# A top-1 expert kernel: the rows 384 to 511 of an expert in float32 blocks of 64 rows, sums of the weights, and a new order

## Chip, cores and metric

The kernel runs on one core of one Trainium2 chip. The metric is the device time of one execution in microseconds (us). The input is one fixed random draw.

## What is computed

Attention in a window of 64 positions (4 batches, 8 heads, 576 positions of 64 channels) gives 2304 tokens of 512 channels. They go through a dense layer pair with `g = h - tanh(h)` (512 to 2048 to 512), and then each token through one of eight experts.

```python
h = x @ w_in                              # 2304 x 512 x 2048
x = (h - np.tanh(h)) @ w_out              # 2304 x 2048 x 512
xn = x / (np.linalg.norm(x, axis=-1, keepdims=True) + 1e-06)
en = expert_emb / (np.linalg.norm(expert_emb, axis=-1, keepdims=True) + 1e-06)
logits = xn @ en.T / tau
expert_idx = np.argmax(logits, axis=1)
...
gate_w = probs[np.arange(N), expert_idx]
for e in range(E):
    mask = expert_idx == e
    h = np.maximum(x[mask] @ w1[e], 0.0)                  # w1[e]: 512 x 1024
    out[mask] = gate_w[mask, None] * (h @ w2[e])          # w2[e]: 1024 x 512
```

With the input of the runs the experts get, in the order in which the kernel takes them, 446, 369, 345, 167, 389, 154, 253 and 181 tokens.

## The kernel before

**Products.** Nearly all products are made of three: an operand is split into a rounded high part and the rest (VectorE subtracts, ScalarE or VectorE rounds), and `mm3` (lines 659 to 662) sums high by high, high by low and low by high. A weight buffer `w` holds the high parts of two 512-column pieces in columns 0 to 1023 and the low parts in 1024 to 2047 (`t_split_w`, line 941). Attention and the token logits use plain float32 products, those of attention on halves of the array (`pv`, line 588, at line 593), those of the logits on quarters (`lg`, line 842, at line 845).

**Order.** A planner, `Sched` (line 83), takes tasks with an engine, a cost, a priority, what they read and write, and the buffers that they need, and writes the instructions of all engines in the order in which they would start. `SHIFTS` is a table of numbers, one for a task, that moves priorities in the first stretch. [...]

**The straight part.** Attention, the dense pair, the routing and the first 256 rows of expert 0 are planned together, up to the first branch (on hardware: to 546 us). The routing (`t_route`, line 784) takes 256 tokens at a time: logits (line 845), turned by line 855, VectorE's choice of the expert (lines 871 to 881), counting products (`ps_`, lines 901 to 904), and a scatter by GpSimd that writes every token's number and gate to its expert's list `lst` (line 927). Lists are loaded by SyncE (`t_list`, line 1333), made into row numbers by VectorE (`t_ids`, lines 987 and 988), and the token rows are gathered by GpSimd (`t_gather`, line 1001) into buffers `v` (rows 0 to 255) or `g` (rows 256 to 511).

**An expert.** Stage e of the loop at line 1467 runs the first 256 rows of expert e (`t_ffn`, line 1074: `h` products of 256 columns, a relu and a split, `o` products of 512 columns), loads and splits the weights of expert e+1, and gathers. `t_out` (line 1112) scales an output by its gate on ScalarE (line 1119) or VectorE (line 1120) into a buffer `pr`, and GpSimd scatters it to `out` (line 1125). Behind that a branch (line 1490, "over") runs the second block, rows 256 to 383, if the expert has over 256 tokens: `t_xin1` (line 1134) transposes and splits the tokens, `t_ffn1` (line 1155) makes `a<-w,x` products, transposes (line 1186), a split (lines 1195 and 1199) and `o<-w,gh` products. Inside it a second branch (line 1501) does the same for the third block, rows 384 to 511. If the first test fails, an Else part prepares the next expert.

```python
with tc.If(vals[e] > CT + P):
    t_ffn1(ws, blk_o, 1, x_o, SC.now)
    SC.run()
```

**The end.** Behind the last expert `nov`, the number of blocks left over (none here), is loaded (line 1584), and a branch (line 1585) jumps over the code for them. [...]

## Time and profile before

| | before |
|---|---|
| median of 3 runs | 808.05 us (807.89 to 809.17) |
| profiled execution | 805.82 us |
| its span | 804.0 us |
| granted TensorE clock, mean | 0.993 |
| busy: TensorE, VectorE, ScalarE, GpSimd | 763.6, 582.8, 472.9, 90.9 us |
| memory traffic over the span | 134 GB/s |

The profile is of one execution. A busy time is the time in which an engine has an instruction in work; an idle time is put down to what ended it. The span runs from the first to the last instruction. In rows of a timeline the time in brackets is idle time ahead of the instruction, with what released it.

### The profile page before, as it was taken

The page shows a single profiled execution, that of the slowest core. Times are in us where ns is not written, and L with a number is a line of the kernel's source. Part 1 is how long each engine was busy: PE and PEld are TensorE (multiplying, and loading weights), DVE is VectorE, ACT ScalarE, POOL GpSimd, SP SyncE. Part 2 cuts the span into 40 slices and gives each one's busy share as a digit, 9 for nine tenths or more (in the row PEclk, how much of TensorE's full clock was granted, in tenths as well). Part 3 has the DMA queues.
Part 4 walks back from the last instruction along what each step waited for, and adds up shares of the span by engine and source line. Part 5 has one row for each costly group of instructions (what it writes and reads, how often), then busy time and mean ns, then how long its engine had stood idle before and what let it go on. Part 6 is the DMA issues. An engine that isn't in the chain of part 4 may idle for free. (4 is left out here: it accounts for less than half of the span.)

```text
span 804.0 us, 15561 instructions
## 1 busy us (share of the span) xinstructions
PE 763.6 (95%) x5703; PEld 672.4 (84%) x5703; DVE 582.8 (72%) x1482; ACT 472.9 (59%) x1121; POOL 90.9 (11%) x116
## 2 busy tenths in 40 slices
PE   4799999999999999999999999998999998999995
PEld 3687888898988789899989889887788888888994
DVE  6999999999988875857668689962282836815761
ACT  6999998889756765645646548721242424423440
POOL 3000000000001210010001011011122122102221
PEclk9999999999999999999999999999999999999998
DMA  9767746566534320200100018635082828523740
GB/s 294 241 188 214 241 148 223 160 216 212 161 106 122 95 80 22 71 1 2 53 1 27 27 34 292 218 61 157 20 247 83 259 62 282 169 82 104 255 132 24
DMA packets 65006, 108.27 MB, mean 135 GB/s; under 512 B 8452, under 2 KB 42244, under 8 KB 64912
## 3 DMA queue, kind: packets, MB, share of 16 engines
q1 hardware_dynamic: 60016, 93.93, 37.1%
q0 software_dynamic: 4896, 13.13, 5.1%
q8 instruction: 54, 0.88, 0.5%
q14 instruction: 40, 0.33, 0.1%
HBM read 88.00 MB, written 20.09 MB: 134 GB/s over the span
## 5 line engine op out<-in xcount | busy, mean ns | idle before, releaser
L660 PE MATMUL h<-x,w 128*128 128x256 f32 x688 | 198.5, 289 | 1.2 <-DVE g L715 1.1
L661 PE MATMUL h<-x,w 128*128 128x256 f32 x688 | 194.7, 283 | 2.0 <-DVE x L635 2.0
L662 PE MATMUL h<-x,w 128*128 128x256 f32 x688 | 194.6, 283 | 1.4 <-DVE w L447 1.4
L660 PE MATMUL o<-w,gh 128*128 128x512 f32 x436 | 175.2, 402 | 0.0
L662 PE MATMUL o<-w,gh 128*128 128x512 f32 x436 | 171.1, 393 | 0.9 <-DVE gh L729 0.7
L661 PE MATMUL o<-w,gh 128*128 128x512 f32 x436 | 170.9, 392 | 0.0
L660 PEld LDWEIGHTS h<-x,w 128*128 128x128 f32 x688 | 131.4, 191 | 8.2 <-issue 2.6
L661 PEld LDWEIGHTS h<-x,w 128*128 128x128 f32 x688 | 131.5, 191 | 4.8 <-DVE x L635 2.2
L662 PEld LDWEIGHTS h<-x,w 128*128 128x128 f32 x688 | 131.4, 191 | 1.6 <-DVE w L447 1.6
L662 PEld LDWEIGHTS o<-w,gh 128*128 128x128 f32 x436 | 81.9, 188 | 21.4 <-DVE gh L729 2.1
L660 PEld LDWEIGHTS o<-w,gh 128*128 128x128 f32 x436 | 82.2, 188 | 16.4 <-issue 2.0
L661 PEld LDWEIGHTS o<-w,gh 128*128 128x128 f32 x436 | 82.3, 189 | 13.8 <-DVE w L447 0.4
L276 ACT CAST w<-st 128x512 fp32r<-128x512 f32 x119 | 72.2, 633 | 22.7 <-DMA st<-in_moe_w_dram 15.2
L950 DVE TENSOR_TENSOR w<-st,w 128x512 fp32r<-128x512 f32 x128 | 83.3, 683 | 0.7
L706 DVE TENSOR_TENSOR g<-h,g 128x512 f32<-128x512 f32 x72 | 49.4, 686 | 29.0 <-ACT g L694 28.9
L1064 ACT ACTIVATE gh<-h 128x256 fp32r<-128x256 f32 x48 | 18.0, 383 | 76.8 <-PE h L662 60.6
L725 ACT CAST gh<-g 128x512 fp32r<-128x512 f32 x72 | 44.0, 620 | 28.3 <-DVE g L719 21.6
L690 ACT ACTIVATE g<-h 128x512 f32<-128x512 f32 x72 | 42.9, 596 | 26.5 <-PE h L662 26.4
L543 ACT ACTIVATE pr<-pr,mx 128x128 f32<-128x128 f32 x144 | 56.1, 401 | 3.2 <-DVE mx L534 3.2
L729 DVE TENSOR_TENSOR gh<-g,gh 128x512 fp32r<-128x512 f32 x72 | 48.6, 683 | 12.9 <-ACT gh L725 12.8
L698 ACT ACTIVATE g<-g,sqa 128x512 f32<-128x512 f32 x72 | 52.3, 726 | 7.2 <-DVE g L719 4.2
L1068 DVE SCALAR_TENSOR_TENSOR gh<-h,gh 128x256 fp32r<-128x256 f32 x48 | 19.8, 420 | 49.5 <-ACT gh L1064 38.6
(205 smaller groups left out, 1366.6 us busy)
## 6 DMA issues: line engine op xcount, KB each, us to landing
st<-in_moe_w_dram SPq DMA_DIRECT2D x64, 512.0 KB
st<-in_moe_w_in_dram SPq DMA_DIRECT2D x16, 512.0 KB
st<-in_moe_w_out_dram SPq DMA_DIRECT2D x16, 512.0 KB
v<-in_v_dram SPq DMA_DIRECT2D x16, 512.0 KB
part<-st SPq DMA_DIRECT2D x11, 512.0 KB
st<-part SPq DMA_DIRECT2D x11, 512.0 KB
k<-in_k_dram SPq DMA_DIRECT2D x16, 320.0 KB
q<-in_q_dram SPq DMA_DIRECT2D x18, 256.0 KB
```

The lines of the kernel that those rows point to most:

```text
L276: return {ACT: (act, lambda: nc.scalar.copy(out=o(), in_=i())), DVE: (dve, lambda: nc.vector.tensor_copy(out=o(), in_=i()))}
L543: nc.scalar.activation(out=pr_.t[:, i, :], in_=pr_.t[:, i, :], func=AF.Exp, bias=st["m"][:, i:i + 1], scale=-1.0, accum_out=st["den"][:, i ...
L660: nc.tensor.matmul(out=ps, lhsT=ah, rhs=bh, start=start, stop=False)
L661: nc.tensor.matmul(out=ps, lhsT=ah, rhs=bl, start=False, stop=False)
L662: nc.tensor.matmul(out=ps, lhsT=al, rhs=bh, start=False, stop=stop)
L690: {ACT: (0.49, lambda: nc.scalar.activation(out=u(), in_=hp.t, func=AF.Square))},
L698: {ACT: (0.62, lambda: nc.scalar.activation(out=sq(), in_=u(), func=AF.Square, scale=SQ_S, bias=sqa))},
L706: {DVE: (0.6, lambda: nc.vector.tensor_tensor(out=th(), in0=hp.t, in1=th(), op=ALU.subtract))},
L725: {ACT: (0.52, lambda: nc.scalar.copy(out=gh(), in_=sq()))}, reads=[(gq, 0), (acc[0], "-"), (acc[1], "-")],
L729: {DVE: (0.6, lambda: nc.vector.tensor_tensor(out=gl(), in0=sq(), in1=gh().bitcast(F32), op=ALU.subtract))},
L950: return lambda: eng.tensor_tensor(out=w.t[:, b], in0=raw.t[:, a], in1=w.t[:, a].bitcast(F32), op=ALU.subtract)
L1068: {DVE: (0.335, lambda: nc.vector.scalar_tensor_tensor(out=part(gs, 1), in0=hp.t[:, 0:CT], scalar=0.0, in1=part(gs, 0).bitcast(F32), op0=A ...
```

## The change

1. **Third block.** The test for rows over 384 now holds a block of 64 rows (`t_ffn_half`), and a test for rows over 448 inside it a second. A block of 64 rows uses plain float32 products with 64 columns of stationary data and 256 moving columns; the two halves of a 512-column row of weights go to output partitions 0 to 63 and 64 to 127, and the output rows, 256 columns wide, are scattered as half rows by numbers that `t_listh` makes.
2. **Sums.** These products need the weights in one piece, so `t_whole` adds high and low parts on VectorE: those of the first layer in the second block, into two `v` and two `pr` buffers; those of the second layer in the third block, into four `g` buffers and, when the first products have read them, the two `v` buffers. The second block's output goes to a `q` buffer.
3. **Hint.** TensorE is told of the test for 384 rows.
4. **End.** `nov` is loaded ahead of the last expert; ScalarE, VectorE and GpSimd are told of the last two branches. In the last expert the last two pieces of the hidden layer are multiplied out half of the rows by half (`last=2`).
5. **Order.** Three planner costs, `FAR` and the whole of `SHIFTS` are new, so all of the straight part stands in a new order.

```diff
-    -617, -89, -188, -90, -232, 135, -108, -84, -118, -93, -65, -74, -74, -76, 12, -30, -48, -70, 95, -705,
+    -1917, -29, -667, -400, -818, -83, -252, -353, -325, -373, -95, -86, -177, -233, 7, 51, -31, 79, 37, -1695,
...
-        SC.add({POOL: (1.04, sc)}, reads=[("su", c), ("pg", c)], writes=[("lst", 0)], prio=pr, lat=2.0)
+        SC.add({POOL: (1.4, sc)}, reads=[("su", c), ("pg", c)], writes=[("lst", 0)], prio=pr, lat=2.4)
...
+            if f < KF2 - last:
+                SC.part()
+                SC.add(
+                    {PE: (1.39, lambda p2=p2: p2((0, 1)))}, reads=rk, writes=[(acc[0], 0), (acc[1], 0)],
+                    allocs=acc if f == 0 and got else [], prio=pr + f + 1.5,
+                )
+            else:
+                ends.append((rk, p2))
         for i in range(2):
+            for rk, p2 in ends:
+                SC.add(
+                    {PE: (0.7, lambda p2=p2, i=i: p2((i,)))}, reads=rk, writes=[(acc[i], 0)], prio=pr + KF2 + i,
+                )
...
+    def t_whole(ws, at, keys, pr, late=()):
+        for n, (j, h) in enumerate(keys):
...
+                nc.vector.tensor_tensor(
+                    out=flat(f)[:, c:c + 512], in0=w.t[:, a].bitcast(F32), in1=w.t[:, b].bitcast(F32), op=ALU.add
+                )
...
+    def t_ffn_half(ws, at, e, b, xr, pr):
+        acc, tm = Buf("o"), []
+        if b:
+            t_whole(ws, at, [(j, h) for j in range(2) for h in range(2)], pr)
...
+            def m1(g=g, ps=ps):
+                for d in range(KD):
+                    for a in range(2):
+                        nc.tensor.matmul(
+                            out=ps.t[sides[a], 0:CT], lhsT=xr.t[:, d * P + b * HB:d * P + (b + 1) * HB],
+                            rhs=full(d, a, g * CT), start=d == 0, stop=d == KD - 1,
+                        )
...
+        t_whole(ws, at, [(j, h) for j in (5, 7) for h in range(2)], pr + 1.5)
...
+            def m2(g=g, gs=gs):
+                for n, (k_, hh) in enumerate(((0, 0), (0, 1), (1, 0), (1, 1))):
+                    f, b0 = hh * 4 + 2 * g + k_, k_ * P + hh * HB
+                    for a in range(2):
+                        nc.tensor.matmul(
+                            out=acc.t[sides[a], 0:CT], lhsT=gs.t[:, b0:b0 + HB],
+                            rhs=full(KD + f // 2, f % 2, a * CT), start=g == 0 and n == 0, stop=g == 1 and n == 3,
+                        )
...
+    def t_ends(e, eng, kind, pr):
+        def go():
+            tc.mark_branch_hint_location(f"over{e}", hint=vals[e] > CT, engines=[kind])
+            tc.mark_branch_hint_location("rest", hint=nov > 0, engines=[kind])
...
-    FAR = 1.5, 3.5
+    FAR = 1.3, 3.7
...
-            t_ffn(ws, blk, x, t0, pre, lead=4.0, got=got)
+            t_ffn(ws, blk, x, t0, pre, lead=4.0, got=got, last=0 if e + 1 < E else 2)
...
-            t_ffn1(ws, blk_o, 0, x_o, t1 + 1.0)
-            t_xin1(blk_o, 1, x_o, t1 + 1.9)
+            tm = t_ffn1(ws, blk_o, 0, x_o, t1 + 1.0)
+            t_xin_half(blk_o, x_r, t1 + 1.9)
...
+            whole = [Buf(n, hold=True) for n in ("v", "v", "pr", "pr", "g", "g")]
+            at = {(j, h): (whole[j], h * 512) for j in range(KD) for h in range(2)}
...
+            t_whole(ws, at, [(j, h) for j in range(KD) for h in range(2)], t1 + LATE, [(x_o, ("q", 0, 1))])
+            SC.add({PE: (0.0, lambda: told(f"past{e}", vals[e] > CT + P))}, reads=[(tm[1], 0)], prio=t1)
             SC.run()
-            with tc.If(vals[e] > CT + P):
-                t_ffn1(ws, blk_o, 1, x_o, SC.now)
+            with tc.If(vals[e] > CT + P, label=f"past{e}"):
+                t_listh(e, SC.now)
+                t_whole(ws, at, [(j, h) for j in (4, 6) for h in range(2)], SC.now + 1.0)
+                t_ffn_half(ws, at, e, 0, x_r, SC.now + 0.1)
                 SC.run()
+                with tc.If(vals[e] > CT + P + HB):
+                    t_ffn_half(ws, at, e, 1, x_r, SC.now)
+                    SC.run()
```

**GpSimd, from the last list scatter to the first branch.** `lst` is the scatter to the lists, `g` a gather for expert 0's second block, `out_dram` a scatter of its first 256 rows. Before:

```order
66 L927 DMA lst<-pg,su 18432x2 [waits DMASW3_49,DMASW2_49,DVE_49]
67 L927 DMA lst<-pg,su 18432x2
68 L1125 DMA out_dram<-pr_7064,idc 2304x512 [waits Activation_49]
69 L1451 TENSOR_LOAD cnti [waits DVE_49]
70 L1001 DMA g_7163<-x2d,gic 128x512 [waits DMAHW6_49,DMAHW5_49,DVE_49]
71 L1001 DMA g_7172<-x2d,gic 128x512 [waits DMASW0_49]
72 L1125 DMA out_dram<-pr_7066,idc 2304x512 [waits DMASW1_49]
73 L1490 COMPARE_AND_BRANCH
```

With the change:

```order
69 L932 DMA lst<-pg,su 18432x2 [waits DMASW3_49,DMASW2_49,DVE_49]
70 L932 DMA lst<-pg,su 18432x2
71 L1006 DMA g_7062<-x2d,gic 128x512 [waits DMAHW6_49,DVE_49]
72 L1604 TENSOR_LOAD cnti [waits DVE_49]
73 L1006 DMA g_7158<-x2d,gic 128x512
74 L1138 DMA out_dram<-pr_7177,idc 2304x512 [waits DMASW0_49,DVE_49]
75 L1138 DMA out_dram<-pr_7175,idc 2304x512 [waits DMASW1_49,Activation_49]
76 L1647 COMPARE_AND_BRANCH
```

Both gathers have moved ahead of both scatters.

**VectorE, second block of expert 0.** `k` is the relu split of the next expert, `x` the split of the tokens, `gh` the split of the hidden layer. Before:

```order
1205 L1068 SCALAR_TENSOR_TENSOR k0_7179<-h0_7051,k0_7179 128x256 [waits Activation_49]
1206 L1068 SCALAR_TENSOR_TENSOR k1_7180<-h1_7071,k1_7180 128x256 [waits Activation_49]
1207 L1150 TENSOR_TENSOR x1_7183<-a0_7182,x1_7183 128x4x128 [waits Activation_49]
1208 L1150 TENSOR_TENSOR x1_7183<-a1_7206,x1_7183 128x4x128 [waits Activation_49]
1209 L1199 TENSOR_TENSOR gh0_7260<-a0_7241,gh0_7260 128x256 [waits PE_49,Activation_49]
```

With the change:

```order
1203 L1073 SCALAR_TENSOR_TENSOR k1_7187<-h0_7044,k1_7187 128x256 [waits Activation_49]
1204 L1073 SCALAR_TENSOR_TENSOR k0_7188<-h1_7143,k0_7188 128x256 [waits Activation_49]
1205 L1163 TENSOR_TENSOR x0_7191<-a2_7190,x0_7191 128x4x128 [waits Activation_49]
1206 L1260 TENSOR_TENSOR v0_7220<-w4_6398 128x512 [waits DMASW6_49,DMASW1_49]
1207 L1260 TENSOR_TENSOR v0_7220<-w4_6398 128x512
1208 L1260 TENSOR_TENSOR v1_7237<-w7_6483 128x512 [waits DMASW7_49,DMASW0_49]
1209 L1260 TENSOR_TENSOR v1_7237<-w7_6483 128x512
1210 L1260 TENSOR_TENSOR pr1_7240<-w0_6249 128x512 [waits DMASW0_49,DVE_49]
1211 L1260 TENSOR_TENSOR pr1_7240<-w0_6249 128x512
1212 L1260 TENSOR_TENSOR pr0_7258<-w1_6252 128x512 [waits DMASW1_49]
1213 L1260 TENSOR_TENSOR pr0_7258<-w1_6252 128x512
1214 L1213 TENSOR_TENSOR gh0_7280<-a2_7261,gh0_7280 128x256 [waits PE_49,Activation_49]
```

Eight additions, the last four behind the scatters from `pr`, stand ahead of the first `gh` split, and one `x` split is gone.

**TensorE, third block of expert 0, between its first and second products.** `a` is a bank of the first products or of the transposes, `o` one of the second. Before:

```order
3688 L660 MATMUL a_7321<-w_6540,x_7183 128x512
3689 L661 MATMUL a_7321<-w_6540,x_7183 128x512
3690 L662 MATMUL a_7321<-w_6540,x_7183 128x512
3691 L1186 MATMUL a_7336<-ident,tmp_7334 128x128 [waits Activation_49]
3692 L1186 MATMUL a_7336<-ident,tmp_7334 128x128 x3
3693 L1186 MATMUL a_7345<-ident,tmp_7341 128x128 [waits Activation_49]
3694 L1186 MATMUL a_7345<-ident,tmp_7341 128x128 x3
3695 L660 MATMUL o_7354<-w_6280,gh_7343 128x512 [waits Activation_49]
3696 L661 MATMUL o_7354<-w_6280,gh_7343 128x512
3697 L662 MATMUL o_7354<-w_6280,gh_7343 128x512 [waits DVE_49]
```

With the change:

```order
3674 L1300 MATMUL a_7346<-v_7220,pT_7215 64x256 [waits PE_49]
3675 L1300 MATMUL a_7346<-v_7220,pT_7215 64x256
3676 L1300 MATMUL a_7346<-v_7237,pT_7215 64x256 x2
3677 L1300 MATMUL a_7346<-pr_7240,pT_7215 64x256 x2
3678 L1300 MATMUL a_7346<-pr_7258,pT_7215 64x256 x2
3679 L1320 MATMUL a_7359<-ident,tmp_7357 128x128 [waits Activation_49]
3680 L1320 MATMUL a_7359<-ident,tmp_7357 128x128
3681 L1320 MATMUL a_7368<-ident,tmp_7363 128x128 [waits Activation_49]
3682 L1320 MATMUL a_7368<-ident,tmp_7363 128x128
3683 L1334 MATMUL o_7372<-g_7158,pT_7366 64x256 [waits DVE_49,Activation_49]
3684 L1334 MATMUL o_7372<-g_7158,pT_7366 64x256
3685 L1334 MATMUL o_7372<-g_7344,pT_7366 64x256 [waits DVE_49]
```

Each `mm3` triple of 512 columns has given way to float32 calls of 256 columns on half of the output partitions, and eight transposes to four.

## Rows read from the trace of the kernel before

**Rows 1.** Page, busy time of each engine (share of the span) and instructions.

```profile
PE 763.6 (95%) x5703; PEld 672.4 (84%) x5703; DVE 582.8 (72%) x1482; ACT 472.9 (59%) x1121; POOL 90.9 (11%) x116
```

**Rows 2.** Windows: length, PE, PEld, DVE, ACT, POOL busy, clock, DMA share, GB/s.

```profile
75.00:300.00 225.00, 220.75 (x1995) 195.86 (x1994) 208.29 (x574) 178.63 (x466) 13.50 (x12) 1.00 0.52 164
300.00:527.00 227.00, 226.56 (x1517) 203.73 (x1516) 171.75 (x363) 136.82 (x260) 16.59 (x17) 1.00 0.22 67
527.00:549.77 22.77, 18.55 (x124) 15.45 (x123) 12.29 (x50) 4.62 (x11) 5.90 (x6) 1.00 0.29 90
...
599.00:804.00 205.00, 191.19 (x1140) 168.10 (x1138) 101.35 (x217) 69.20 (x149) 40.98 (x40) 0.98 0.47 148
```

**Rows 3.** Waits of TensorE: us in total, times, longest.

```profile
PE a L1140 <- DMA g<-x2d,gic: 3.9, 1, 3.9
```

**Rows 4.** Windows of the two third blocks (experts 0 and 4).

```profile
566.86:579.25 12.39, 12.14 (x57) 9.74 (x56) 1.61 (x4) 3.17 (x7) 0.99 (x1) 1.00 0.06 21
...
718.12:730.53 12.41, 12.16 (x57) 9.74 (x56) 1.61 (x4) 3.18 (x7) 0.97 (x1) 1.00 0.06 21
```

**Rows 5.** Half-array calls (line 593, one group), quarter-array calls (line 845, timeline).

```profile
L593 PE MATMUL a<-pT,v x32: 222/222/270, 289.7 to 290.6; 128*64 128x64 f32 x32
...
527.83 0.28 PE L662 MATMUL h<-x,w 128*128 128x256 f32 x1
528.04 0.64 PE L845 MATMUL a<-st,enT 128*32 128x256 f32 x8
528.61 0.50 PE L660 MATMUL o<-w,gh 128*128 128x512 f32 x1
```

**Rows 6.** TensorE's timeline between the products of expert 0's third block.

```profile
572.30 0.60 PE L1186 MATMUL a<-ident,tmp 128*128 128x128 f32 x4
...
573.56 0.49 PE L660 MATMUL o<-w,gh 128*128 128x512 f32 x1
```

**Rows 7.** Group of ScalarE: busy us, mean ns | idle before, releaser.

```profile
L1064 ACT ACTIVATE gh<-h 128x256 fp32r<-128x256 f32 x48 | 18.0, 383 | 76.8 <-PE h L662 60.6
```

**Rows 8.** Group of VectorE.

```profile
L950 DVE TENSOR_TENSOR w<-st,w 128x512 fp32r<-128x512 f32 x128 | 83.3, 683 | 0.7
```

**Rows 9.** GpSimd's timeline ahead of the first branch.

```profile
543.29 0.97 POOL L1125 DMA_INDIRECT out_dram<-pr,idc  x1 [5.36 <-ACT pr L1119]
...
546.01 0.97 POOL L1001 DMA_INDIRECT g<-x2d,gic  x1 [0.30 <-issue]
547.28 1.02 POOL L1125 DMA_INDIRECT out_dram<-pr,idc  x1 [0.30 <-issue]
```

**Rows 10.** Window behind the wait of rows 3.

```profile
549.77:553.20 3.43, 3.43 (x17) 3.43 (x18) 0.69 (x1) 0.59 (x1) 0.00 (x0) 0.52 0.92 240
```

**Rows 11.** Timelines of VectorE and TensorE around the last choice and count.

```profile
532.14 0.17 DVE L871 TENSOR_TENSOR l<-a,nrm 128x16 f32<-128x16 f32 x1
...
533.25 0.17 DVE L881 TENSOR_TENSOR oh<-eq,m 128x16 bf16<-128x16 f32 x1
...
533.84 0.17 PE L904 MATMUL a<-oh,upper 128*128 128x8 bf16 x1
```

**Rows 12.** Line 1585, the last branch: duration ns min/median/max, first and last start.

```profile
L1585 POOLq EVENT_SEMAPHORE  x4: 17/43/43, 800.2 to 800.5; - x4
...
L1585 PEldq COMPARE_BRANCH  x1: 3832/3832/3832, 795.2 to 795.2; - x1
...
L1585 POOLq COMPARE_BRANCH  x1: 45/45/45, 797.3 to 797.3; - x1
```

**Rows 13.** Expert 4's second block: DMA queue from 703.5 to 708.8, and VectorE's timeline.

```profile
q0 software_dynamic: 160, 0.52, 24.3%
...
711.69 0.43 DVE L1199 TENSOR_TENSOR gh<-a,gh 128x256 fp32r<-128x256 f32 x1 [3.98 <-ACT gh L1195]
```

**Rows 14.** Line 1125, all scatters of the output.

```profile
L1125 POOL DMA_INDIRECT out_dram<-pr,idc x22: 972/1008/1859, 543.3 to 796.3; - x22
```

**Rows 15.** TensorE's timeline behind the branch of expert 3.

```profile
675.75 0.28 PE L660 MATMUL a<-x,w 128*128 128x256 f32 x1 [2.44 <-issue]
```

More of the change, by code (lines that the diff above doesn't have):

```diff
@@ L233, in attn_moe_moe2 @@
     CAP = 512
+    HB = P // 2
+    LATE = 3.5
     SCALE = 1.0 / float(D) ** 0.5
@@ L1072, in t_relu, with t_ffn @@
         )
-    def t_ffn(ws, blk, x, pr, pre=(), line=None, lead=0.0, got=()):
+    def t_ffn(ws, blk, x, pr, pre=(), line=None, lead=0.0, got=(), last=0):
         _, st, lb_, uid = blk
-        acc = [Buf("o") for _ in range(2)]
+        acc, ends = [Buf("o") for _ in range(2)], []
         for f in range(KF2):
@@ new lines, in flat, with t_xin_half, tr @@
+    def flat(f):
+        return f.t.rearrange("p a b -> p (a b)")
+    def t_xin_half(blk, xr, pr):
+        r, ps = blk[0][1], Buf("a")
+        def tr():
+            for d in range(KD):
+                nc.tensor.transpose(out=ps.t[:, d * P:(d + 1) * P], in_=rows(r)[:, d * P:(d + 1) * P], identity=ident)
+        SC.add({PE: (0.43, tr)}, reads=[(r, 0)], writes=[(ps, 0)], allocs=[ps, xr], prio=pr)
+        SC.add({ACT: (0.48, lambda: nc.scalar.copy(out=xr.t, in_=ps.t))}, reads=[(ps, 0)], writes=[(xr, 0)], prio=pr)
```

125 lines of the change are left out of this document (104 added, 21 removed), and 70 rows, old and new, of the table SHIFTS.

## Prediction

> **What bounds the kernel now.** I read first the busy line of the page [rows 1]: TensorE has work in 95% of the 804.0 us span, VectorE in 72%, ScalarE in 59%. The table of windows [rows 2] shows that this is no mean over like stages: from 75 to 527 us TensorE idles 4.7 of 452 us, while 4.2 us of idle time lie between 527 and 549.77 and 13.8 behind 599. The waits of TensorE [rows 3] name the longest hole of the expert part: 3.9 us for gathered rows of expert 0. So a change pays if it takes work from TensorE in the expert part or closes such a hole; what it does to VectorE, ScalarE and GpSimd counts only where TensorE comes to wait for it. The profiled execution took 805.82 us, 1.8 more than its span; the runs have a median of 808.05. I work against 805.82 and add the difference, 2.2, at the end.
>
> **Term 1, the third blocks (rows 384 to 511).** The inputs send 446 rows to expert 0 and 389 to expert 4, all others get fewer than 384. These two blocks take 12.39 and 12.41 us [rows 4]: 48 products of 512 columns and eight transposes each. In the change one block of 64 rows is enough for either (62 and 5 rows are left), and the test for the other half fails. Its work is 32 float32 products of 256 columns in 16 pairs, the two of a pair on different halves of the output partitions.
> A pair's price has two near rows. In attention, 16 calls of this form with 64 columns leave 32 records, four to a pair, that start from 289.7 to 290.6 [rows 5]: 0.9 us for eight pairs, 0.11 to 0.12 each, so four times as many columns cost 0.45 to 0.48. In the routing, four calls of 256 columns, each on a quarter of the output partitions, start at 528.04 and the next other product at 528.61 [rows 5]: 0.57 us. I take 0.47 for a pair, by the attention rows, which use the same halves; 0.57 is the dear end. Sixteen pairs are 7.5 us.
> Between the first products and the second stand transposes and a copy. Before, the first transpose started at 572.30 and the first product on its result at 573.56 [rows 6], 1.26 us; now two transposes, 0.2 us less, stand ahead of a ScalarE operation on the same 256 columns, 0.38 us [rows 7]. I take 1.1. At the end ScalarE scales 256 columns before the next expert gets that bank: 0.6 with the handover. Together 7.5 + 1.1 + 0.6 = 9.2 us against 12.4, so **3.2 us less in each, -6.4 in both**. With 0.57 a pair it would be 10.8 and -3.2, with 0.45 8.9 and -7.0.
> Four times in a block TensorE changes between products on the whole array and on its halves. In the routing a whole product starts at 527.83 and the quarter products 0.21 us later [rows 5], where whole ones of this size follow each other at 0.12; one change costs about 0.1, and I leave four of them to the margin. [...]
> VectorE makes the sums of weights that these products read: eight additions in every second block (experts 0, 1, 2, 4 run one), eight more in a third. The nearest row is an addition of the same size, 0.68 us [rows 8]. In a third block four are done ahead of the second products; four wait until the first products have read their buffers, at 3.8 us, and end 2.7 us later, at 6.5, when the second products have come about to the half that needs them. I put that at nothing; were they late, the block would grow by it, some tenths.
>
> **Term 2, the way into expert 0's second block.** Before, GpSimd issued a scatter at 543.29, then two gathers, the last at 546.01, then the other scatter [rows 9]. [...] In the new order GpSimd issues both gathers ahead of both scatters, some 1.3 us earlier, and more work of TensorE is left to cover them: 36 products of 512 columns and 72 of 256 stand between the last counting product and the branch, 16.8 us at steps of 0.23 and 0.12. Before it was 12.0 us, from the counting at 533.84 [rows 11] to 545.83; the lists, their ids and the gathers took 15.9, to 549.77. So the wait and the slow clock should both go, 5.6 us. Against that, 6 products (1.4 us) now stand between the last token logits and the counting, where 18 (2.9 us) hid VectorE's choice of the expert. That chain took from 532.14 to 533.25 [rows 11], behind up to 1.3 us of other work on VectorE. I charge 0.8. **Term 2 is -4.8**; its ends are -5.6 and +1 (gathers still late, choice bare).
>
> **Term 3, the end.** Behind the last scatter GpSimd's branch over the rest block starts at 797.3, and its next instruction comes at 800.2; TensorE's takes 3.83 us from 795.2 [rows 12]. In the change the number of rest blocks is loaded earlier and the branch is announced on GpSimd, VectorE and ScalarE, and the last two pieces of the hidden layer are multiplied out by halves of rows, so that one half of the output is complete six products (1.4 us) earlier. TensorE is not told, and its branch still ends near 799. GpSimd can gain most of its 2.9 us, but not beyond TensorE's. **Term 3 is -2**, between -0.5 and -3.
>
> **What I cost at nothing.** Ahead of 527 us the same products stand on TensorE in another order; with 4.7 us idle from 75 to 527 it can win little and lose what its new waits cost, and I allow 5 us either way. The eight additions of a second block, 5.5 us, replace one split of 0.69 and fall into stretches in which VectorE waits, some 7 us in each.
>
> Sum: -6.4 - 4.8 - 2.0 = -13.2, so 792.6 for a profiled execution and **795 us** as a median.
>
> **Rivals.**
> *The halves run one after the other.* Then a pair costs two calls of 0.47, and a third block 16 x 0.94 + 1.7 = 16.7 us, 4.3 more than before, +8.6 for both in place of -6.4: 810, slower. It decides from 0.67 us a pair on, where the block costs what it did. Against it speak the eight pairs in 0.9 us [rows 5], for it that no row shows 256 columns in this form. Chance 0.05.
> *The additions hold up the second blocks.* Two of the sums stand in the buffers from which the main part's output is scattered, so they wait for these scatters to land, and VectorE's splits for the second products stand behind them in its order. For expert 4 all 160 packets of the scatters lie before 708.8 and the first split is at 711.69 [rows 13]; two additions take 1.4, which leaves 1.5 us. If scatters land later than that, TensorE waits for the rest of it in four blocks; at 2 us each, +8: 803. Chance 0.10. Scatters take GpSimd 0.97 to 1.86 us to issue [rows 14], with additions of this kind beside some of them. [...]
> *The wait at expert 0 stays, or comes back in the choice.* Term 2 is 0 or a little more: 800. Chance 0.15.
> *A code fetch moves.* Behind the branch of expert 3 TensorE stood 2.44 us for nothing but its instructions [rows 15] and then ran slowly, some 4 us in all, where experts 5 and 6 go the same way without. The code lies elsewhere now: this may go (791) or come twice (799). Chance 0.10 for each.
> *The new order ahead of 527 us is worse by 10 to 15 us*, through waits of products for decoded weights: 805 to 810. Chance 0.08.
>
> **How the numbers follow.** The forecast has 0.42, the fetch that goes 0.10, the rivals from 799 to 803 0.35, the halves 0.05 and the worse order 0.08, half of which ends at no change. The lower end of the range takes the terms at their best (-7.0 - 5.6 - 3.0) and most of the 5 us of the new order or of the fetch: 785. The upper end takes term 1 at -3.2, term 3 at -0.5, none of term 2 and nothing else: 804, rounded to 805. Some 0.2% of the time, 1.6 us, is what a measurement of this kernel can tell from no change. Faster 0.87, within it 0.04, slower 0.09.
>
> **What would show it.** Right: third blocks of about 9.2 us at experts 0 and 4, in two stretches of 3.8; no wait for the gather ahead of expert 0's second block and a full clock behind it; GpSimd's first instruction behind the last branch within 1 us. Wrong: pairs over 0.57 us; TensorE waiting in a second block for VectorE's splits; a new wait of over 3 us ahead of 527; a total above 805.

## The result, and the profile after

The changed kernel takes 793.38 us (median of 4 runs, 793.03 to 795.06), the kernel before on the same chip 807.97 (807.84 to 809.17): a ratio of 0.982, 95% interval 0.9803 to 0.9837. Forecast were 795.0, from 785 to 805. The profiled execution took 793.28 us with a span of 791.6; 805.82 and 804.0 before. I compare these two executions by stages, each from the first product of its kind on TensorE to that of the next stage:

| stage | before | after | difference |
|---|---|---|---|
| start to expert 0's second block | 549.77 | 545.82 | -3.95 |
| expert 0, second block | 17.08 | 16.14 | -0.94 |
| expert 0, third block | 12.40 | 8.82 | -3.58 |
| expert 3 and its Else part | 27.63 | 23.54 | -4.09 |
| expert 4, third block | 12.42 | 8.96 | -3.46 |
| expert 6 and its Else part | 23.38 | 25.70 | +2.32 |
| last product to the end of the span | 9.76 | 11.29 | +1.52 |
| all others together | | | -0.2 |

The busy line of the page: TensorE has 10.4 us less than in [rows 1], VectorE 21.4 more, with the sums.

```profile
PE 753.2 (95%) x5727; PEld 662.2 (84%) x5727; DVE 604.2 (76%) x1516; ACT 474.4 (60%) x1124; POOL 94.2 (12%) x118
```

Windows of the changed kernel, columns as in [rows 2]: the straight part in two pieces, and expert 0's second and third blocks.

```profile
75.00:300.00 225.00, 222.78 (x1961) 198.53 (x1960) 208.58 (x558) 180.54 (x460) 12.50 (x12) 1.00 0.53 164
300.00:523.00 223.00, 222.54 (x1552) 199.66 (x1550) 170.03 (x375) 135.87 (x266) 19.47 (x17) 1.00 0.21 67
...
545.82:561.96 16.14, 15.91 (x89) 13.40 (x87) 9.98 (x20) 4.78 (x11) 2.00 (x2) 1.00 0.40 144
561.96:570.78 8.82, 8.09 (x69) 4.82 (x68) 3.26 (x7) 2.65 (x6) 0.97 (x1) 1.00 0.08 32
```

From 75 to 300 us TensorE idles 2.2 us, where it idled 4.3. The clock in the second block is 1.00; behind its start it was 0.52 [rows 10]. GpSimd's timeline shows why there is no gather to wait for: both gathers are issued by 540.10, the last of them 5.9 us earlier than in [rows 9], and the scatters follow.

```profile
538.75 0.99 POOL L1006 DMA_INDIRECT g<-x2d,gic  x1 [7.86 <-DVE idc L993]
540.10 0.96 POOL L1006 DMA_INDIRECT g<-x2d,gic  x1 [0.36 <-issue]
546.36 1.01 POOL L1138 DMA_INDIRECT out_dram<-pr,idc  x1 [5.30 <-DVE pr L1133]
```

TensorE's timeline through expert 0's third block. Each call leaves two records, so 32 records are 16 calls, or 8 pairs.

```profile
561.64 0.39 PE L667 MATMUL o<-w,gh 128*128 128x512 f32 x1
561.96 1.08 PE L1300 MATMUL a<-v,pT 128*64 128x256 f32 x8
...
564.60 1.03 PE L1300 MATMUL a<-pr,pT 128*64 128x256 f32 x8
565.57 0.99 PE L1320 MATMUL a<-ident,tmp 128*128 128x128 f32 x4
566.49 1.95 PE L1334 MATMUL o<-g,pT 128*64 128x256 f32 x16
568.27 1.90 PE L1334 MATMUL o<-v,pT 128*64 128x256 f32 x16
570.78 0.50 PE L665 MATMUL o<-w,k 128*128 128x512 f32 x1 [0.62 <-ACTq L1669]
```

Its two stretches of products, and those of expert 4, as windows:

```profile
561.96:565.57 3.61, 3.61 (x34) 2.21 (x33) 1.96 (x5) 1.07 (x2) 0.97 (x1) 1.00 0.19 73
...
566.49:570.06 3.57, 3.57 (x33) 2.21 (x32) 0.38 (x1) 0.37 (x1) 0.00 (x0) 1.00 0.02 5
...
705.58:709.19 3.61, 3.61 (x34) 2.21 (x33) 1.96 (x5) 1.07 (x2) 0.97 (x1) 1.00 0.19 73
710.11:713.68 3.57, 3.57 (x33) 2.21 (x32) 0.38 (x1) 0.37 (x1) 0.00 (x0) 1.00 0.02 5
```

Eight pairs in 3.6 us are 0.45 us a pair. Between the stretches lie 0.92 us, behind the second 0.72. VectorE's timeline in the same block: the second four sums wait for the first products to have read the `v` buffers and end at 566.87, ahead of the products that need them (568.27).

```profile
560.10 2.49 DVE L1260 TENSOR_TENSOR g<-w 128x512 f32<-128x512 f32 x4
...
564.37 2.50 DVE L1260 TENSOR_TENSOR v<-w 128x512 f32<-128x512 f32 x4 [1.65 <-PE a L1300]
```

Three things are new on the other side. One is a wait for the choice of the experts of the last tokens. Timelines of ScalarE, VectorE and TensorE: a weight piece lands late, ScalarE's cast waits for it, VectorE's split (line 955) waits for the cast, and the choice (lines 876 to 886) stands behind the split in VectorE's order.

```profile
523.68 1.14 ACT L278 CAST w<-st 128x512 fp32r<-128x512 f32 x2 [3.77 <-DMA st<-in_moe_w_dram]
```

```profile
524.33 1.29 DVE L955 TENSOR_TENSOR w<-st,w 128x512 fp32r<-128x512 f32 x2 [2.12 <-ACT w L278]
525.54 0.17 DVE L876 TENSOR_TENSOR l<-a,nrm 128x16 f32<-128x16 f32 x1
...
526.66 0.17 DVE L886 TENSOR_TENSOR oh<-eq,m 128x16 bf16<-128x16 f32 x1
```

```profile
526.89 0.17 PE L909 MATMUL a<-oh,upper 128*128 128x8 bf16 x1 [2.06 <-DVE oh L886]
```

That wait costs more than its 2.06 us. Behind it, from 527 to 531 us, TensorE runs at a granted clock of 0.58. In `order_only` (below), which has the same order, the wait is 1.98 us and the clock stays at 1.00. This window of the changed kernel and of `order_only`:

```profile
527.00:531.00 4.00, 3.91 (x23) 3.72 (x22) 3.23 (x18) 1.84 (x4) 2.01 (x2) 0.58 0.03 7
```

```profile
527.00:531.00 4.00, 3.96 (x29) 3.71 (x30) 3.55 (x20) 1.65 (x3) 2.00 (x2) 1.00 0.01 2
```

From the end of the wait to the start of the second block the same products take 18.93 us here and 17.57 in `order_only`: I put the 1.36 us between them down to the slow clock.

The second is a stop of TensorE behind expert 6's branch, 2.07 us that end by nothing that the profile shows; an instruction packet of 16 KB moves from 755.42 to 756.45, while that branch is in work (3.46 us from 754.39). The third is the end. Groups of lines 1647 (the branches over the second blocks) and 1757 (over the rest); duration min/median/max in ns, first and last start:

```profile
757.91 0.39 PE L665 MATMUL a<-x,w 128*128 128x256 f32 x1 [2.07 <-issue]
```

```profile
L1647 PEldq COMPARE_BRANCH  x8: 76/266/3902, 542.4 to 779.1; - x8
...
L1757 POOLq EVENT_SEMAPHORE  x4: 17/42/43, 784.5 to 788.0; - x4
...
L1757 POOLq COMPARE_BRANCH  x1: 70/70/70, 782.8 to 782.8; - x1
L1757 PEldq COMPARE_BRANCH  x1: 5070/5070/5070, 783.2 to 783.2; - x1
```

TensorE's jump behind the last expert takes 3.90 us (the longest of line 1647), the next 5.07, where the last one alone took 3.83 [rows 12]. GpSimd's branch starts at 782.81 and its next instruction comes at 784.5, 1.7 us later where it was 2.9 [rows 12]. But it then stands until 788.0 for the landing of the second scatter. GpSimd's timeline and the DMA view from 782 to 790 us (queue: packets, MB, share of 16 engines; and issues with the median from issue to landing):

```profile
781.00 1.01 POOL L1138 DMA_INDIRECT out_dram<-pr,idc  x1 [15.98 <-ACT pr L1132]
782.30 1.00 POOL L1138 DMA_INDIRECT out_dram<-pr,idc  x1 [0.30 <-issue]
```

```profile
q8 instruction: 3, 0.05, 3.7%
...
out_dram<-pr,idc POOLq DMA_INDIRECT x2, 4.6
```

Three instruction packets of 16 KB move in these 8 us. Two of them run from 783.72 for 1.45 us and from 784.62 for 2.24 us, and scatter packets start just as these end, at 785.15 and 786.83; the last ends at 787.19. That these fetches are TensorE's, and that the scatter packets queue behind them, is inferred from the times: TensorE's jump lasts from 783.17 to 788.24. The scatter lands 5.62 us behind its issue. So the end is set by its landing, not by GpSimd's branch.

Before, the landing was close to setting the end too. Of the two scatters, packets still moved from 799.0 to 800.3 us (queue: packets, MB, share):

```profile
q0 software_dynamic: 4, 0.01, 2.1%
```

The trace has the last update of the second scatter's semaphore at 799.93, 3.66 us behind its issue and 0.3 ahead of GpSimd's next instruction at 800.21. So of the 2.9 us at GpSimd's branch only some 0.3 could be won without an earlier landing.

### The profile page after: what moved, and what is told of

Read it like the earlier page. It is cut to its first block, busy times and chain, and to the rows that moved or that the text cites. A ratio compares the mean times of both kernels' runs of the same rounds, so it can differ in the third digit from the quotient of the medians.

```text
span 791.6 us, 15770 instructions
## 1 busy us (share of the span) xinstructions
PE 753.2 (95%) x5727; PEld 662.2 (84%) x5727; DVE 604.2 (76%) x1516; ACT 474.4 (60%) x1124; POOL 94.2 (12%) x118
## 5 line engine op out<-in xcount | busy, mean ns | idle before, releaser
L665 PE MATMUL o<-w,gh 128*128 128x512 f32 x420 | 169.4, 403 | 0.0
L667 PE MATMUL o<-w,gh 128*128 128x512 f32 x420 | 164.4, 391 | 1.0 <-DVE gh L734 0.7
L666 PE MATMUL o<-w,gh 128*128 128x512 f32 x420 | 164.6, 392 | 0.0
L667 PEld LDWEIGHTS o<-w,gh 128*128 128x128 f32 x420 | 78.9, 188 | 20.4 <-DVE gh L734 1.7
L665 PEld LDWEIGHTS o<-w,gh 128*128 128x128 f32 x420 | 79.2, 189 | 16.4 <-issue 2.8
L666 PEld LDWEIGHTS o<-w,gh 128*128 128x128 f32 x420 | 79.3, 189 | 12.8 <-DVE w L452 0.4
L1073 DVE SCALAR_TENSOR_TENSOR gh<-h,gh 128x256 fp32r<-128x256 f32 x48 | 19.9, 421 | 55.3 <-ACT gh L1069 54.8
```

Of the source, the lines that this page charges most:

```text
L665: nc.tensor.matmul(out=ps, lhsT=ah, rhs=bh, start=start, stop=False)
L666: nc.tensor.matmul(out=ps, lhsT=ah, rhs=bl, start=False, stop=False)
L667: nc.tensor.matmul(out=ps, lhsT=al, rhs=bh, start=False, stop=stop)
L1073: {DVE: (0.335, lambda: nc.vector.scalar_tensor_tensor(out=part(gs, 1), in0=hp.t[:, 0:CT], scalar=0.0, in1=part(gs, 0).bitcast(F32), op0=A ...
```

## The experiments

All medians and ratios are against the kernel before on the same chip, run beside them (its medians: 808.84 for the first four kernels, 809.60 for the next four, 808.15 for the three after them, 810.05 for the last).

| kernel | median, us | ratio, 95% interval | span |
|---|---|---|---|
| order_only | 801.00 | 0.9900 (0.9873 to 0.9927) | 796.9 |
| half_only | 799.87 | 0.9887 (0.9861 to 0.9913) | 796.6 |
| end_only | 806.64 | 0.9986 (0.9968 to 1.0004) | 804.2 |
| no_end | 793.56 | 0.9799 (0.9773 to 0.9825) | 791.9 |
| pe_told | 792.73 | 0.9811 (0.9774 to 0.9849) | 789.8 |
| unpaired | 797.37 | 0.9875 (0.9835 to 0.9914) | 795.6 |
| one_half | 794.18 | 0.9827 (0.9787 to 0.9866) | 792.0 |
| choice | 796.05 | 0.9848 (0.9813 to 0.9882) | 794.2 |
| choice_first | 791.81 | 0.9804 (0.9773 to 0.9834) | 794.2 |
| pad | 794.68 | 0.9849 (0.9819 to 0.9878) | 792.1 |
| both | 791.02 | 0.9795 (0.9765 to 0.9824) | 789.3 |
| late_half | 796.00 | 0.9822 (0.9798 to 0.9847) | 796.3 |

**The parts alone.** `order_only` is the kernel before with the new table, costs and `FAR`, and nothing else.

```diff
-    -617, -89, -188, -90, -232, 135, -108, -84, -118, -93, -65, -74, -74, -76, 12, -30, -48, -70, 95, -705,
+    -1917, -29, -667, -400, -818, -83, -252, -353, -325, -373, -95, -86, -177, -233, 7, 51, -31, 79, 37, -1695,
...
-    FAR = 1.5, 3.5
+    FAR = 1.3, 3.7
```

> The kernel before with the new order alone (the table, the three planner costs, FAR). Theory (the terms are separate): expert 0's second block begins near 546 us instead of 549.8, with no wait for the gather and a full clock behind it, so this stretch gives some 4.9 us; third blocks stay at 12.4 us and the end (from the start of the last expert's products, 26.3 us before) stays as it is; total near 0.994 of before, unless a code fetch behind a branch moves (2 to 4 us either way). Rival: the new order gains only together with the other parts, because the straight part itself is slower; then the second block begins at 548 or later and the ratio is 0.998 to 1.00.

The second block starts at 544.26 us and takes 16.06; the third blocks take 12.42 each. TensorE has no wait for a gather, and the clock is full behind the start:

```profile
548.00:551.50 3.50, 3.50 (x17) 2.88 (x16) 0.07 (x1) 0.60 (x1) 0.00 (x0) 1.00 0.82 314
```

So term 2 belongs to the order alone: -5.5 and -1.0 here; the full change, with the slow clock behind the choice, has -3.95 and -0.94. The ratio, 0.9900, is better than the 0.994 expected: the stop behind expert 3 is shorter too (1.65 us, and 25.36 for the stage). The end did not stay as it was: from the start of the last expert it takes 27.16 us, where it was 26.28.

`half_only` is the other half: the blocks of 64 rows and the sums, with the old order and the old end.

```diff
-            t_ffn(ws, blk, x, t0, pre, lead=4.0, got=got, last=0 if e + 1 < E else 2)
+            t_ffn(ws, blk, x, t0, pre, lead=4.0, got=got)
...
-    FAR = 1.3, 3.7
+    FAR = 1.5, 3.5
```

> The kernel before with the blocks of 64 rows and the sums alone (old order, old end). Theory: third blocks 8.8 to 9.0 us in place of 12.4, 7.0 to 7.5 us in both with what follows them; the wait of 3.9 us into expert 0's second block stays. For the end: if the longer code of the blocks is what makes TensorE's jump over the last expert's second block slow, that branch takes 3 to 4 us here (0.34 before) and the last stretch is 1 us or more longer than 26.3; ratio near 0.992. Rival (the edits of the end make that jump slow): the branch stays below 0.5 us and the last stretch at 26.3; ratio near 0.991.

The third blocks take 8.82 and 8.96, as in the full change. The wait for the gather is still there:

```profile
PE a L1153 <- DMA g<-x2d,gic: 3.8, 1, 3.8
```

Its branches stall as those of the full change do: 3.69 us in expert 6, 3.69 and 4.46 behind the last expert, and the stop in expert 3 is gone (23.54). From the start of the last expert to the end it takes 26.81 us, so 0.5 more than before where the theory had 1 or more. In these runs the stops in expert 6 and at the first jump behind the last expert come with the code of the new blocks, then, without the edits at the end.

`end_only` is the kernel before with the edits of the end.

```diff
-            t_ffn(ws, blk, x, t0, pre, lead=4.0, got=got)
+            t_ffn(ws, blk, x, t0, pre, lead=4.0, got=got, last=0 if e + 1 < E else 2)
...
-    with tc.If(nov > 0):
+    with tc.If(nov > 0, label="rest"):
```

> The kernel before with the edits of the end alone. Theory (the longer code of the blocks makes TensorE's last jumps slow): TensorE's branch over the last second block stays at 0.3 to 0.5 us, its last branch at some 3.8, GpSimd is through its last branch within 1 us, and the last stretch of 26.3 us falls by 1 to 2.5; ratio 0.997 to 0.999. Rival (these edits themselves make the jumps slow, by fetches of the other engines at the same time): TensorE's branch over the last second block takes 3 us or more and the last stretch grows to 27 or more; ratio 1.000 to 1.002.

From the start of the last expert to the end it takes 25.58 us, 0.7 less than before (26.28); TensorE's jump behind the last expert stays under 0.5 us and the next takes 3.79. The total, 0.9986 (0.9968 to 1.0004), can't be told from no change.

`no_end` is the changed kernel without them (the same lines the other way round).

> The changed kernel without the edits of the end. Theory (longer code): TensorE's branch over the last second block still takes 3 to 4 us and the last stretch is as long as in the changed kernel (27.8 us) or longer by what GpSimd then loses at its own last branch; total 793 to 796. Rival (the edits of the end cost it): the branch is back below 0.5 us, the last stretch at 26.3, total near 791.9.

The same stretch takes 27.17 us, in the full change 27.81, and TensorE's jump behind the last expert still 3.67. With the longer code the edits of the end thus give nothing (0.6 us worse in one profiled execution each).

**Pairs.** `unpaired` issues all calls to one half of the output partitions ahead of those to the other; the work is the same.

```diff
-                for d in range(KD):
-                    for a in range(2):
+                for a in range(2):
+                    for d in range(KD):
```

> The changed kernel with the same products in the 64-row blocks, but all of one half of the output partitions ahead of all of the other, so that neighbours use the same half of the array. Theory (a pair costs 0.44 us because its halves run beside each other): each call then costs the 0.44 us of a pair, the two stretches of products take 7.0 to 7.2 us each in place of 3.6, and a third block 15.8 to 16.2 us in place of 8.8; total 14 us above the changed kernel, about as long as before. Rival (the price of 0.44 us is that of two calls in a row anyway): third blocks stay at 8.8 to 9.5 us.

The third blocks take 10.86 and 10.99 us: neither the 15.8 to 16.2 of the theory nor the 8.8 to 9.5 of the rival. TensorE's timeline shows why it is between:

```profile
560.30 1.08 PE L1300 MATMUL a<-v,pT 128*64 128x256 f32 x4
561.22 0.38 PE L1300 MATMUL a<-pr,pT 128*64 128x256 f32 x1
561.23 0.43 PE L1300 MATMUL a<-v,pT 128*64 128x256 f32 x1
561.43 0.38 PE L1300 MATMUL a<-pr,pT 128*64 128x256 f32 x1
561.49 0.38 PE L1300 MATMUL a<-v,pT 128*64 128x256 f32 x1
...
563.98 1.03 PE L1300 MATMUL a<-pr,pT 128*64 128x256 f32 x4
```

The first four records are two calls of one half alone; they take 0.92 us up to the next, 0.46 a call. Then calls on the other half (from `v` again) start while two calls on the first half (from `pr`), which stand ahead of them, are only beginning, and run beside them. A call alone costs what a pair costs (0.46 and 0.45 us), so it is pairing that makes the block 8.8 us, and written pairs beat what TensorE pairs by itself by 2.0 us a block.

**The jumps.** `pe_told` tells TensorE too of the last two branches, in the middle of the last expert.

```diff
-            for eng, kind in ((ACT, mybir.EngineType.Activation), (DVE, mybir.EngineType.DVE), (POOL, mybir.EngineType.Pool)):
+            for eng, kind in ((PE, mybir.EngineType.PE), (ACT, mybir.EngineType.Activation), (DVE, mybir.EngineType.DVE), (POOL, mybir.EngineType.Pool)):
```

> The changed kernel, with TensorE too told of the last two branches in the middle of the last expert, in place of the one announcement directly ahead of the branch. Theory (TensorE's two late jumps make the end long, and their fetches hold up the last packets of the second scatter): TensorE's branches take below 0.5 us and below 1.5 us in place of 3.90 and 5.07, GpSimd's wait for the scatter ends within 2.5 us of its issue (5.6 before), and the last stretch falls from 27.8 to 24.5 to 25.5 us; total some 2.5 us lower than the changed kernel. Rival (the second announcement replaces the first, or the fetched code is lost before the branch): one of the two branches stays at 3.5 us or more and the last stretch falls by less than 1 us.

The jumps still take 3.54 and 3.12 us, but the second scatter lands 3.86 us behind its issue where it was 5.62, and the end comes 9.52 us behind the last product where it was 11.29. So neither side holds: one jump stays above 3.5 us, as the rival has it, but the last stretch falls by 1.8 us, to 26.05. Announcing does not take the stops away here, but the end is shorter with it. In the six kernels that have the end of the full change (`unpaired`, `choice`, `choice_first`, `pad` and `late_half` beside it) the scatter lands 5.4 to 5.9 us behind its issue and the end comes 11.1 to 11.6 us behind the last product; `both`, below, has the early announcement too, and 3.48 and 9.15. The total is 0.65 us below that of the full change, which the intervals don't tell apart.

`one_half` leaves out the code for rows 448 to 511 (no expert here has so many, but that part of the computation is missing).

```diff
-                with tc.If(vals[e] > CT + P + HB):
-                    t_ffn_half(ws, at, e, 1, x_r, SC.now)
-                    SC.run()
```

> The changed kernel without the code for rows 448 to 511 (no expert of this input has that many), so that the same work runs in shorter code. Theory (the length of the code that a jump has to pass decides): TensorE's branch over the last second block falls from 3.90 to below 0.5 us, that of expert 6 from 3.46 to below 0.5, though the stall may come back behind another expert as before; last stretch 26 to 26.5 us; total 2 to 4 us below the changed kernel. Rival (the second block's own additions and the sums' code are long enough, or the edits of the end decide): both branches stay above 3 us, total within 1 us.

The stop in expert 6 and the first behind the last expert are gone (the second takes 3.92 us, near the 3.83 of [rows 12]), and one has come at the end of expert 2's second block (3.61 us; the block takes 22.43 where it was 19.41). The second of these groups has it, line 1664, the branch over the third block:

```profile
L1647 PEldq COMPARE_BRANCH  x8: 76/220/468, 542.8 to 781.9; - x8
```

```profile
L1664 PEldq COMPARE_BRANCH  x8: 75/218/3607, 560.7 to 717.5; - x8
```

Expert 3 takes 26.36 us where it was 23.54, but no jump stops there: behind the stop of expert 2, which ends at 648.98, TensorE runs 6 us at a granted clock of 0.50, and that costs about 3.

```profile
649.00:655.00 6.00, 6.00 (x14) 4.76 (x15) 0.00 (x0) 0.00 (x0) 2.85 (x3) 0.50 0.55 161
```

`pad` puts 32 more transposes into each of these never entered parts.

```diff
-                for k_ in range(2):
+                for k_ in (0, 1) * (1 + 16 * b):
```

> 32 more transposes stand in each expert's part for rows 448 to 511 that no expert of this input enters: the same work is executed, the code behind them lies at other addresses. Theory (where the code lies decides which untaken jumps stall TensorE): the stalls of 3.46 us in expert 6, and of 3.90 and 5.07 us behind the last expert, are not all there again, or others appear in experts 1 to 5; stages without a moved stall stay within 0.3 us; total anywhere between 788 and 800 us. Rival (the length of the jump, or which engines are told of it, decides): the three stalls stay at 3.4 to 5.1 us in the same places, none appears elsewhere, total 793 to 795 us.

Both hold in part: the three stops stay (3.44, 3.71 and 4.93 us), and two smaller ones come in experts 2 (1.65; the stage is 1.2 us longer) and 4 (1.84, which costs nothing: the third block takes 8.82). That left open whether a stop goes with the length of its own jump or with what stands ahead, and `late_half` was made for it: the part for rows 448 up is left out (and missing) in experts 0 to 5 only.

```diff
-                with tc.If(vals[e] > CT + P + HB):
-                    t_ffn_half(ws, at, e, 1, x_r, SC.now)
-                    SC.run()
+                if e >= 6:
+                    with tc.If(vals[e] > CT + P + HB):
+                        t_ffn_half(ws, at, e, 1, x_r, SC.now)
+                        SC.run()
```

> The code for rows 448 to 511 is left out in experts 0 to 5 and kept in experts 6 and 7, so the jumps over the blocks of experts 6 and 7 are as long as in the changed kernel, while the code ahead of them is as short as in the kernel without that part anywhere. If the length of its own jump decides a stall: the jump in expert 6 takes 3.4 to 3.9 us, that behind the last expert 3.5 to 3.9 and the one behind it 4.9 to 5.3, and experts 2 and 3 stall as in the kernel without that part (22.4 and 26.4 us stages). If the code's place decides: one or more of expert 6's and 7's stalls is under 1 us, or their places differ from both kernels.

```profile
L1647 PEldq COMPARE_BRANCH  x8: 76/266/3982, 544.8 to 783.9; - x8
```

```profile
L1664 PEldq COMPARE_BRANCH  x8: 75/218/3204, 562.7 to 719.4; - x8
```

Experts 2 and 3 take 22.21 and 26.36 us, as in `one_half`: a jump of 3.20 us in expert 2, and the clock at 0.50 behind it. Expert 6 does not stop (23.36), although its jump is as long as in the full change, where it stopped: its length alone does not decide there, and what stands ahead in the code does. Behind the last expert both jumps take what they did in the full change (3.98 and 5.10 us). There length and place aren't told apart by these runs.

**The wait for the choice.** `choice` gives the planner 1.4 us more for the choice, so that 18 products stand ahead of the counting as before, in place of 6.

```diff
-        SC.add({DVE: (1.23, n1)}, reads=[(at_, 0), ("nrm", c)], writes=[("oh", c)], prio=pr)
+        SC.add({DVE: (1.23, n1)}, reads=[(at_, 0), ("nrm", c)], writes=[("oh", c)], prio=pr, lat=1.4 if c + 1 == NC else 0.0)
```

> The changed kernel with 1.4 us added to the planner's cost of the last choice of the expert, which puts 18 products ahead of the last counting step in place of 6. Theory (the 2.1 us wait of TensorE for the choice is a pure loss): that wait falls below 0.5 us, expert 0's second block starts 1.5 to 2 us earlier, 544 in place of 545.8, without a wait for its gathered rows; total some 2 us lower. Rival (the lists then come later and the gathers again decide): a wait for the gather of 1 us or more comes back and the second block starts within 0.5 us of 545.8.

A miss: the wait for the choice is gone, but TensorE waits 2.8 and 1.2 us for `gh` (line 1073) instead, since VectorE's order is what it was. The second block starts at 546.74, later than in the full change. `choice_first` leaves TensorE's order and puts VectorE's split of the late weight piece behind the choice.

```diff
-            t_split_w(ws[j], raw, (raw, 0), pr(j))
+            t_split_w(ws[j], raw, (raw, 0), pr(j), [("oh", NC - 1)] if (i, j) == (1, 5) else [])
```

> The VectorE split of the weight piece that arrives late is put behind the choice of expert 0's over rows; every other order stays. Theory (VectorE's order is what delays the choice, the number of TensorE products is not): VectorE's choice chain no longer stands behind the 2.12 us wait for ScalarE's part of that weight, the 2.1 us wait of TensorE's counting product for the choice falls below 0.5 us, expert 0's second block starts at 543.5 to 544.5 us instead of 545.82, total 791 to 792 us. Rival: the weight split that now comes later, or the lists, hold TensorE for the same two microseconds in another place: start of the second block at 545.5 to 547, total 793 to 795 us.

In the profiled execution the second block starts at 546.23, as the rival has it. The choice is now done early, and TensorE waits next for ScalarE's part of `gh`, which stands behind the cast of the same late piece on ScalarE. Timelines of VectorE, ScalarE and TensorE:

```profile
524.18 0.17 DVE L886 TENSOR_TENSOR oh<-eq,m 128x16 bf16<-128x16 f32 x1
```

```profile
525.71 1.14 ACT L278 CAST w<-st 128x512 fp32r<-128x512 f32 x2 [6.12 <-DMA st<-in_moe_w_dram]
```

```profile
527.64 0.39 PE L665 MATMUL h<-x,w 128*128 128x256 f32 x1 [2.99 <-DVE gh L1073]
```

So the theory named only half of it: the order delays the choice, but the late load is behind both waits. In this profiled execution the piece came 2.0 us later than in that of the full change; the execution, 795.96 us, is the slowest of this kernel's five, whose median, 791.81, is where the theory has it. In the seven kernels with the full change's order the wait for the choice follows the start of that cast: 1.3 us of wait with the cast at 523.13 (`unpaired`), 2.1 at 523.68 (the full change), 2.5 at 523.94, 2.4 at 524.06, 2.3 at 524.16, 3.0 at 524.56 and 3.3 at 525.16 (`late_half`). Whether the clock falls behind the wait does not follow its length, if the time from the wait to the second block tells it: that takes 17.6 us behind waits of 1.3 us (`unpaired`), 1.98 (`order_only`, at a granted clock of 1.00) and 2.4 (`pad`), 18.9 behind 2.1 (the full change, 0.58), 2.3, 2.5 and 3.0, and 19.9 behind 3.3.

`both` joins `choice_first` and `pe_told`.

> The changed kernel with the VectorE split behind the choice and with TensorE among the engines that are told early of the last expert's two jumps. If both gains hold and add up (2 us at the choice, 0.65 us behind the last expert): 790 to 791.5 us. If the split only moves the wait, or a jump's stall moves to another expert with the new addresses: 793 us or more.

With the cast at 524.27 TensorE's longest wait is 1.0 us, where that landing cost 2.3 to 2.5 with the old order of VectorE:

```profile
526.20 0.39 PE L665 MATMUL h<-x,w 128*128 128x256 f32 x1 [1.05 <-DVE gh L1073]
```

The second block starts at 543.95. In `pad`, with the cast 0.2 us earlier, the 17.6 us of a full clock and the old order of VectorE, it starts at 544.83, so the order gives some 0.9 us; the rest of the distance to the full change's 545.82, 1.0 us, I put down to its slow clock. The end comes 9.15 us behind the last product. At 791.02 us, 0.9795 (0.9765 to 0.9824), it is the fastest here, but its interval overlaps that of the full change (0.9803 to 0.9837), so that it is faster than that isn't shown.

## Why the prediction was right, and where it was not

**Term 1, forecast -6.4, measured -7.0** (-3.58 and -3.46). Mechanism and size hold: a pair costs 0.45 us where I took 0.47, the way between the stretches 0.92 where I took 1.1, the end 0.72 where I took 0.6. The rows of attention [rows 5] gave the right price and the quarter calls the wrong one, and `unpaired` shows the cause: a call alone costs 0.46. The change of mode has a row now: the first call on halves starts 0.32 us behind the last whole product where whole ones follow each other at 0.23, so about 0.1 as estimated, which is no reason against mixing the two in this block.

**Term 2, forecast -4.8, measured -4.9** (-3.95 and -0.94), and `order_only` shows it to be the order's alone. The wait for the gather and the slow clock behind it went, as forecast. No run shows the 1.7 us by themselves that the sum has for the clock beside the wait of 3.94, an estimate from 3.43 us at 0.52 [rows 10]: with the clock at 1.00 the second block takes 16.06 us in `order_only` where it took 17.08, 1.0 less. That the size came out is luck: the choice was sized at 0.8 and cost 3.4, 2.06 of waiting and 1.36 at the slow clock. I allowed 1.3 us for other work of VectorE ahead of the choice, but not that this work, a split, itself waits for a load, and not that the clock would fall again. The straight part made up for it; from 75 to 300 us it idles 2.0 us less, and the rest, some 1.4 us, I can't assign.

**Term 3, forecast -2, measured +1.5** from the last product on. Three steps failed. The first is "one half of the output is complete six products (1.4 us) earlier". The trace shows the order at the end of the changed kernel: VectorE's split of the last piece, the third of TensorE's last four groups of three products (from 777.76, 778.46, 779.15 and 779.83), and ScalarE's scaling of the output:

```profile
778.38 0.42 DVE L1073 SCALAR_TENSOR_TENSOR gh<-h,gh 128x256 fp32r<-128x256 f32 x1 [2.40 <-ACT gh L1069]
```

```profile
779.15 0.39 PE L665 MATMUL o<-w,gh 128*128 128x512 f32 x1
```

```profile
780.03 1.37 ACT L1132 ACTIVATE pr<-o,lb 128x512 f32<-128x512 f32 x2 [1.68 <-PE o L667]
```

The last split ends at 778.80, so the two groups ahead of that belong to the last piece but one, one for each half of the rows. The third group completes the first half, which ScalarE scales from 780.03, and the fourth the second. So the first half is complete three products ahead, as it was, and the first scatter starts 0.71 us behind the start of the last product (781.00 and 780.28), as before. I read the loop where I should have read the order. The second is "GpSimd can gain most of its 2.9 us": its next instruction came 1.3 us sooner (not within 1 us of the branch, the sign that I gave, but at 1.7), but before, the second scatter landed just 0.3 us ahead of that instruction, so no more than that was there to win. `end_only` has 0.7 in one execution, and there too GpSimd waits for that scatter at the end. The third is "its branch still ends near 799": I took TensorE's jumps as given while the code around them grew, and beside them the scatter landed 5.62 us behind its issue in place of 3.66. That alone is more than the 1.5.

**At nothing.** The sums never held TensorE up; in expert 0's second block the first `gh` split stands directly behind them, so the rival fell with nothing to spare. I had counted two sums behind the scatters from `pr`, 1.4 us, where the order has four, 2.5 us as measured; that leaves 0.4 us of the room and not 1.5. The fetch was a rival with 0.10 each way (a 16 KB instruction packet moves from 672.75 to 674.35, in the stop of [rows 15]), and it went both ways: gone in expert 3 (-4.09), come in expert 6 (+2.32) and, through the scatter, in the end. Together these and the end are -0.2, so the sum, -12.4 by the spans where I had -13.2, came out by terms 1 and 2. That is luck in part: term 3 was 3.5 us worse than forecast, and stops of -1.8 us together, which my sum left out, and 0.7 us in terms 1 and 2 stand against it. That the profiled execution of before lies 2.2 us under its median and that of after 0.1 is not explained; the medians are 14.6 apart. The lower end of the range was added up wrong: the terms at their best give 792.4, and less the whole 5 us it would be 787.4, not 785. The result lies inside either.

**What stays open.** Which of TensorE's jumps stop, and by how much, I can't say ahead. Instruction packets of 16 KB move in stops (from 755.42 in expert 6's, from 783.72 and 784.62 in the last), but one also moves from 664.04, behind a jump of expert 3 that takes 0.46 us from 662.63 and stops nothing; no run shows what a stop waits for. `late_half` shows only that what stands ahead in the code can decide. `pe_told` shows that announcing the jumps early does not take the stops away (3.54 and 3.12 us in place of 3.90 and 5.07). Nor can I say when the clock falls behind a wait: with the same order the way to the second block took 17.6 us behind a wait of 2.4 us and 18.9 behind one of 2.1.

## What to carry to other kernels

Plain float32 products on 64 output partitions were worth it in these short blocks (8.8 and 9.0 us in place of 12.4), written in pairs on the two halves; a pair cost 0.45 us and a call alone 0.46, so price a pair as one call. As code inside untaken branches grew here, jumps that the edit didn't touch took 3.2 to 5.1 us, in places that the next edit moved again; so judge an edit by the stages it touches rather than by the total. Behind a wait of two microseconds look at the clock as well: here, behind 2.06 us, the way on took 1.36 us more at a granted clock of 0.58. Ahead of the end ask when the last scatter lands before you shorten what runs beside it. Before you count on products to hide a chain, read what stands ahead of that chain on its own engine, and read the recorded order rather than the loop.

## What the runs showed of the hardware

- In `unpaired` TensorE started calls on one half of its output partitions ahead of earlier calls on the other: a record from `v` starts at 561.23, ahead of records from `pr` at 561.43 and later that stand before it in the program. So the order of execution was not the program order there.
- Some jumps over untaken code took TensorE 1.65 (`pad`) to 5.10 us (`late_half`) in the kernels above, most others under 0.5.
- Instruction packets of 16 KB took 1.45 and 2.24 us at the end of the changed kernel. The scatter whose packets start as these end landed 5.6 us after its issue; the same scatter took 3.2 to 4.5 in eight of the other kernels, and 5.4 to 5.9 in five (`unpaired`, `choice`, `choice_first`, `pad` and `late_half`).
- A stop of two microseconds in expert 6 was followed by a granted clock of 1.00 in the changed kernel (from 759 to 763 us), but by 0.57 over 4 us in `choice_first` (27.39 us for the stage in place of 25.70). Of the nine kernels that stop there, five have 25.7 to 26.0 us for the stage and four (`unpaired`, `choice`, `choice_first`, `both`) 27.2 to 27.5, with idle times of 2.05 to 2.36 and 2.09 to 2.43 us, so the length of the stop does not tell which:

```profile
760.00:764.00 4.00, 4.00 (x24) 4.00 (x23) 0.78 (x2) 0.77 (x2) 0.00 (x0) 0.57 0.18 65
```
